# Pairing two chunks of the q·k products by accumulating DMA before the logit matmuls of a fused attention and gMLP kernel

## The chip, the cores and the metric

The kernel runs on one core of one Trainium2 chip. The metric is the device time of one execution in microseconds (us); lower is better. A run is quoted as the median of its executions. All comparisons use runs of the fast state; where a kernel also had executions in the slow state (e6_plain and e9_plainload), only the fast ones are quoted.

## The reference, cut to what matters

The input x (2048 tokens, 512 features, bf16) is normalised and then goes two ways at once, and both results are added to x:

```python
# A: attention with 32 heads of 16 features; each token sees 8 tokens, 2 apart
idx = pos[:, None] - arange(8) * 2
logits = einsum('bhsd,bhswd->bhsw', q, kg) * scale      # dot products over 16 features
attn = softmax(where(mask, logits, -1e9))
o = einsum('bhsw,bhswd->bhsd', attn, vg) @ wo
# B: gMLP
z = gelu(xn @ w_in); z1 = z[..., :688]; z2 = layernorm(z[..., 688:])
g = einsum('ts,bsf->btf', w_sp, z2) + b_sp              # w_sp is 2048 x 2048
out = x + o + (z1 * g) @ w_out
```

The change concerns only the logits. The large matmul with w_sp, called `pg` in the kernel, comes after them on the same engine.

## The kernel before

q and k come out of TensorE with the features on the 128 partitions, in four chunks of 128 features (8 heads each). VectorE multiplies q by shifted k. TensorE then sums the 16 features of each head: it multiplies the products by a 0/1 matrix `rsel`, and each chunk has its own matrix, which puts its 8 heads into its own 8 of 32 output rows. The four chunks add up in PSUM. The work is split into eight groups (four token blocks, two halves of the window), `prods(g)` and `logits(g)`.

```python
def qk_part(pq, j, c, b0, b1):                # chunk c of q (s=0) and k (s=1)
    for s in range(2):
        for kc in range(C):
            PE.matmul(pq[:, s, b0 * P:b1 * P], wqk[:, kc, s * D + c * P:s * D + (c + 1) * P],
                      xv[:, kc, b0:b1, j, :], start=(kc == 0), stop=(kc == C - 1))

def prod_w(g, ww):                            # one of four window positions, all four chunks
    V.tensor_tensor(pr[g % 2][:, :, ww], q4, k4, ALU.mult)

def logits(g):
    for c in range(C):                        # C = 4
        for tb in range(TB):                  # TB = 4
            PE.matmul(pl[32 * tb:32 * tb + 32, :, :], rsel[:, c, :], pr[g % 2][:, c, :, tb, :],
                      start=(c == 0), stop=(c == C - 1), tile_position=(0, 32 * tb))
    A.activation(lg[...], pl[:], ACT.Copy, scale=float(DH) ** -0.5)

# ... (the order of issue, cut)
SP.dma_start_transpose(b16[:], B_b_sp...)     # the bias column, late in the SyncE queue
G.tensor_copy(b_col[:], b16[:])               # GpSimd: waits for it
for c in range(C):
    prod_c(0, c)                              # groups 0 and 1, chunk by chunk
    prod_c(1, c)
# ...
logits(7)
add_mask()
sm_max(1)
z2s(3, 1)
z2s(3, 2)
for n in range(NWSP):
    load_wsp(n)                               # six DMA transposes of w_sp, from SyncE
# ...
```

`r_qk` holds q and k, and the w_sp tiles are written over it later: so the first six transposes wait until VectorE has made the last products.

## Time and profile before

The median is 210.8 us (210.47 to 211.88) before the prediction.

| read from | number |
|---|---|
| page, busy time | PE 202.7 of 209.3 us, 97% |
| page, chain | PE 93% of the span |
| groups | logit matmuls `pl`, 128 of them, 8.2 us |
| chain | `pg` starts at 83.5 us; PE is busy without gaps from there |
| timelines | GpSimd casts the bias at 35.9 us; w_sp transposes go out from 69.5 us |

From the page of the kernel before. First the span and the busy time by engine; then the span in 40 slices of 5.2 us, each digit the busy share in tenths (`PEclk`: the granted TensorE clock); then the chain of work that ended last, by engine; then two groups (line, engine, operation, out<-in, count, busy us, mean ns, and idle time before them with its releaser):

```profile
span 209.3 us, 4186 instructions
...
PE 202.7 (97%) x1727; PEld 121.3 (58%) x1731; DVE 176.9 (85%) x267; ACT 92.9 (44%) x148; POOL 5.7 (3%) x21
...
PE   7799999999999999999999999999999999999993
...
PEclk9999999999999999999999999999999999999999
DMA  4984556000000499799999776994833234424153
...
PE 93%; DMA 3%; SPq 2%; issue 1%; DVE 0%; DVEq 0%
...
L297 DVE TENSOR_TENSOR r_pr<-r_qk 128x2048 bf16<-128x2048 bf16 x24 | 27.5, 1218 | 2.8 <-ACT r_qk L269 2.8
L264 PEld LDWEIGHTS <-r_w 128*128 128x128 bf16 x176 | 16.8, 98 | 11.5 <-issue 1.8
```

TensorE is the limit, at full clock. The DMA row is empty between about 37 and 68 us: that is the room in which the change wants to work. VectorE, which makes the products, is the next engine (85%).

From the groups of the same trace, the logit matmuls, in the same columns:

```profile
L304 PE MATMUL pl<-r_pr,rsel 128*32 128x512 bf16 x128 | 8.2, 381 | 0.0
```

Nothing waits here, so 8.2 us is all that logit matmuls can give back, and half of it is what the change is after.

From the chain in order of time (start us, us, what), the stretch up to `pg`:

```profile
69.43 2.44 PE pz L207 x16
72.85 3.61 PE pz L207 x24
76.45 7.07 PE pv L342 x128
83.52 18.77 PE pg L377 x128
```

From the timelines of GpSimd and of SyncE (start us, us, engine, line, operation, count, idle time before and releaser):

```profile
35.92 1.05 POOL L540 CAST b_col<-b 128x16 f32<-128x16 bf16 x1 [30.43 <-DMA b<-in_B_b_sp_dram]
...
69.51 16.15 SPq L369 DMA_TRANSPOSE r_qk<-in_B_w_sp_dram  x6
```

The cast waits 30 us for its DMA and delays nobody. The six transposes go out the moment the last products are read.

### The profile page before, as it was taken

Reading aid. Unit: us, or ns where it says so; the run is one execution under the profiler, and the core shown is the slowest. Engines: PE = TensorE matmul, PEld = TensorE weight load, DVE = VectorE, ACT = ScalarE, POOL = GpSimd, SP = SyncE. Lnnn points to the kernel's source line nnn. Section 1 sums busy time; section 2 is a strip of 40 time slices with the busy share of each in tenths; the row PEclk is TensorE's granted clock in tenths of the full one; section 3 lists DMA queues with packets and bytes.
Section 4 is the critical chain, followed back from the end, with each engine's and each line's share of the span. In section 5 each row is a group of like instructions: output and inputs, shape, how many; then the busy total and the mean of one; then the engine's idle time right before and its main releaser. Section 6 shows DMA issues by size and latency. Waiting matters only on the chain.

```text
span 209.3 us, 4186 instructions
## 1 busy us (share of the span) xinstructions
PE 202.7 (97%) x1727; PEld 121.3 (58%) x1731; DVE 176.9 (85%) x267; ACT 92.9 (44%) x148; POOL 5.7 (3%) x21
## 2 busy tenths in 40 slices
PE   7799999999999999999999999999999999999993
PEld 2578644545566566666666666456666446664441
DVE  3888997969999987999999999859999979991404
ACT  3475797788997897941431223102123102231000
POOL 7000001100000000000000000000000000000000
PEclk9999999999999999999999999999999999999999
DMA  4984556000000499799999776994833234424153
GB/s 132 326 281 66 101 94 232 0 0 3 0 3 0 103 179 210 146 280 216 177 191 218 129 161 145 147 194 150 126 76 89 47 94 150 47 45 89 51 152 100
DMA packets 66914, 25.91 MB, mean 124 GB/s; under 512 B 56080, under 2 KB 66768, under 8 KB 66768
## 3 DMA queue, kind: packets, MB, share of 16 engines
q1 hardware_dynamic: 66304, 25.20, 56.1%
q10 hardware_dynamic: 592, 0.46, 0.7%
q8 instruction: 13, 0.21, 0.4%
q14 instruction: 5, 0.04, 0.1%
HBM read 10.13 MB, written 2.10 MB: 58 GB/s over the span
## 4 chain that ended last, share of the span: by engine, by line
PE 93%; DMA 3%; SPq 2%; issue 1%; DVE 0%; DVEq 0%
PE pg L377 36%; PE pz L207 18%; PE pq L264 12%; PE po L430 7%; PE po L411 7%; PE pv L342 7%; PE pl L304 4%; DMA r_w<-in_A_wqkv_dram 3%; PE pa L430 1%; PE po L417 1%; SPq L138 1%; SPq L131 1%; SPq L147 0%; PE pt L193 0%; DVE r_qk L422 0%
## 5 line engine op out<-in xcount | busy, mean ns | idle before, releaser
L377 PE MATMUL pg<-z,r_qk 128*128 128x344 bf16 x512 | 76.8, 309 | 0.0
L377 PEld LDWEIGHTS <-r_qk 128*128 128x128 bf16 x512 | 50.0, 98 | 24.9 <-issue 0.4
L207 PE MATMUL pz<-w_z,xnT 128*128 128x344 bf16 x256 | 40.9, 309 | 0.0
L380 ACT ACTIVATE gs<-pg,b_col 128x688 bf16<-128x688 f32 x16 | 13.3, 832 | 57.0 <-PE pg L377 50.1
L353 DVE TENSOR_TENSOR r_pr<-r_x,r_w 128x2048 bf16<-128x2048 bf16 x32 | 38.1, 1221 | 0.3
L357 DVE TENSOR_TENSOR r_pr<-r_pr 128x2048 bf16<-128x2048 bf16 x28 | 33.8, 1219 | 0.1
L207 PEld LDWEIGHTS <-xnT 128*128 128x128 bf16 x256 | 24.6, 98 | 14.7 <-issue 2.0
L264 PE MATMUL pq<-xnT,r_w 128*128 128x256 bf16 (+1 forms) x176 | 29.4, 321 | 0.8 <-ACT xnT L197 0.7
L297 DVE TENSOR_TENSOR r_pr<-r_qk 128x2048 bf16<-128x2048 bf16 x24 | 27.5, 1218 | 2.8 <-ACT r_qk L269 2.8
L264 PEld LDWEIGHTS <-r_w 128*128 128x128 bf16 x176 | 16.8, 98 | 11.5 <-issue 1.8
L422 DVE TENSOR_TENSOR r_qk<-po,r_qk 128x512 bf16<-128x512 f32 x14 | 9.0, 686 | 15.6 <-PE po L430 15.6
L256 ACT ACTIVATE z1u<-pz 128x688 bf16<-128x688 f32 x16 | 11.9, 742 | 20.8 <-PE pz L207 20.7
L269 ACT CAST r_qk<-pq 128x1024 bf16<-128x1024 f32 x16 | 15.8, 1012 | 5.8 <-PE pq L264 4.3
L430 PE MATMUL po<-r_w,uT 128*128 128x512 bf16 x66 | 14.9, 379 | 0.6 <-issue 0.6
L342 PE MATMUL pv<-xnT,r_w 128*32 128x512 bf16 x256 | 14.7, 380 | 0.0
L411 PE MATMUL po<-r_lg,r_pr 32*128 32x512 bf16 x224 | 14.5, 375 | 0.0
L430 PEld LDWEIGHTS <-uT 128*128 128x128 bf16 x80 | 7.5, 98 | 10.2 <-issue 1.7
L175 DVE BATCH_NORM_STATS2 stats<-r_x 128x6 f32<-128x512 bf16 x16 | 10.8, 672 | 2.3 <-DMA r_x<-in_A_x_dram 2.1
L219 ACT ACTIVATE junk<-z 128x688 bf16<-128x688 bf16 x16 | 12.4, 778 | 0.5
L213 ACT ACTIVATE z<-pz 128x688 bf16<-128x688 f32 x16 | 11.8, 736 | 1.9 <-PE pz L207 1.9
L342 PEld LDWEIGHTS <-r_w 128*32 128x32 bf16 x256 | 9.5, 139 | 4.5 <-issue 0.3
L411 PEld LDWEIGHTS <-r_pr 32*128 32x128 bf16 x256 | 6.2, 93 | 7.7 <-issue 1.3
(67 smaller groups left out, 136.3 us busy)
## 6 DMA issues: line engine op xcount, KB each, us to landing
r_lg<-in_A_wo_dram SPq DMA_DIRECT2D x4, 512.0 KB, 9.0
r_qk<-in_A_x_dram SPq DMA_DIRECT2D x16, 128.0 KB, 2.2
out_dram<-r_qk SPq DMA_DIRECT2D x15, 128.0 KB, 1.7
r_x<-in_A_x_dram SPq DMA_DIRECT2D x3, 512.0 KB, 6.0
w_z<-in_B_w_in_dram SPq DMA_DIRECT2D x2, 688.0 KB, 5.3
r_w<-in_A_wqkv_dram SPq DMA_DIRECT2D x4, 256.0 KB, 6.4
r_w<-in_B_w_out_dram SPq DMA_DIRECT2D x1, 640.0 KB, 5.6
r_w<-in_A_wqkv_dram SPq DMA_DIRECT2D x1, 512.0 KB, 4.0
```

Of the source, the lines that this page charges most:

```text
L207: PE.matmul(pz[:, hh, 0:FHALF], xnT[:, kc, i * P:(i + 1) * P], wz[:, kc, hh * FHALF:(hh + 1) * FHALF], start=(kc == 0), stop=(kc == C - 1))
L219: A.activation(junk[:], z2[:, i, :], ACT.Square, accum_out=zsq[:, q:q + 1])
L264: PE.matmul(pq[:, s, b0 * P:b1 * P], wqk[:, kc, s * D + c * P:s * D + (c + 1) * P], xv[:, kc, b0:b1, j, :], start=(kc == 0), stop=(kc == C ...
L269: A.copy(dst[:, :, :, j, :], pq[:].rearrange("p s (b t) -> p s b t", b=TB))
L297: V.tensor_tensor(pr[g % 2][:, :, ww], q4, k4, ALU.mult)
L342: PE.matmul(pv[32 * tb:32 * tb + 32, dd, :], wv[:, kc, 2 * d2 + dd, :], xnT[:, kc, tb * TBS:(tb + 1) * TBS], start=(kc == 0), stop=(kc == ...
L353: V.tensor_tensor(pw_t[n], vp[:, :, off:off + P], a_sb[:, slot_w(w), ts].unsqueeze(1).broadcast_to([P, DH, P]), ALU.mult)
L357: V.tensor_tensor(pw_t[n] if dst is None else dst, pw_t[n], pw_t[m], ALU.add)
L377: PE.matmul(pg[:, hh, 0:FHALF], wsp[n % NWSP][:, k, :], z2[:, k, hh * FHALF:(hh + 1) * FHALF], start=(q == 0), stop=(q == NT - 1))
L380: A.activation(gs[:], pg[:, :, 0:FHALF], ACT.Identity, bias=b_col[:, i:i + 1])
L411: PE.matmul(pos[tb], op[32 * tb:32 * tb + 32, d, o * P:(o + 1) * P], wo_r[32 * tb:32 * tb + 32, d, :], start=(d == 0), stop=False, tile_po ...
L430: PE.matmul(pos[tb], uT[:, o % 2, m, tb * P:(tb + 1) * P], wout[:, m, :], start=False, stop=(m == MCH - 3))
```

## The change: its intent and its diff

If the features are dealt to chunks by stride 4 (chunk c takes features c, c+4, c+8, ...), then every chunk holds four features of every head, all four chunks need the same 0/1 matrix, and chunks may be added before it. An accumulating DMA, issued by GpSimd, adds chunks 2 and 3 to chunks 0 and 1 inside SBUF. The logits then need 8 matmuls a group, not 16. To give the DMAs time, a third product buffer is made and the logits are moved later in TensorE's order. Core of the diff:

```diff
-    pr = [r_pr[:, n * 8192:(n + 1) * 8192]... for n in range(2)]
+    pr_home = [r_pr[:, 0:8192], r_pr[:, 8192:16384], r_uz[:, (NZ1 + 8) * FPAD - 8192:]]   # three buffers
+    pr = [h.rearrange("p (w c b t) -> p w c b t", w=4, c=C, b=TB) for h in pr_home]
 # load order: all of q, then all of k, then x block 1 (before: half of q and k, x block 1, the other half)
     load_wqk(SP, 0)
+    load_wqk(SP, 1)
     SP.dma_start(xall[:, 1], xblk[1])
-    load_wqk(SP, 1)
 # qk_part
-                PE.matmul(..., wqk[:, kc, s * D + c * P:s * D + (c + 1) * P],
+                PE.matmul(..., wqk[:, kc, s * D + c:(s + 1) * D:C],
+    def pair_c(g, c):
+        p = pr[g % 3]
+        G.dma_start(p[:, :, c].rearrange("p w b t -> p w (b t)"),
+                    p[:, :, c + 2].rearrange("p w b t -> p w (b t)"), accum_op=ALU.add)
+    def pair_w(g, w0):
+        p = pr[g % 3][:, w0:w0 + 2].rearrange("p w c b t -> p w (c b t)")
+        G.dma_start(p[:, :, 0:1024], p[:, :, 1024:2048], accum_op=ALU.add)
 # logits
-        for c in range(C):
+        for c in range(2):
-                PE.matmul(..., rsel[:, c, :], pr[g % 2][:, c, :, tb, :], start=(c == 0), stop=(c == C - 1), ...)
+                PE.matmul(..., rsel[:], pr[g % 3][:, :, c, tb, :], start=(c == 0), stop=(c == 1), ...)
 # prods: after every second window position
+            if ww % 2:
+                pair_w(g, ww - 1)
 # order of issue (start)
     for c in range(C): qk_mm(2, c)
-    logits(0)
-    logits(1)
     prods(2)
-    prods(3)
     qk_mm(3, 0) ... qk_mm(3, 2)
+    logits(0)
+    logits(1)
+    prods(3)
 # ... the later logits move back in the same way; v_mm and z1_mm pieces are moved ahead of them (cut)
```

More of the change, by code (lines that the diff above doesn't have):

```diff
@@ L99 @@
     r_pr = sb.tile([P, 2 * 4 * C * TB * P], BF16, name="r_pr")
-    pr = [r_pr[:, n * 8192:(n + 1) * 8192].rearrange("p (c w b t) -> p c w b t", w=4, c=C, b=TB) for n in range(2)]
+    r_uz = sb.tile([P, (NZ1 + 8) * FPAD], BF16, name="r_uz")
+    z1u = r_uz[:, 0:NZ1 * FPAD].rearrange("p (n f) -> p n f", n=NZ1)
+    uT = r_uz[:, NZ1 * FPAD:(NZ1 + 8) * FPAD].rearrange("p (s m t) -> p s m t", s=2, m=MCH)
+    pr_home = [r_pr[:, 0:8192], r_pr[:, 8192:16384], r_uz[:, (NZ1 + 8) * FPAD - 8192:]]
+    pr = [h.rearrange("p (w c b t) -> p w c b t", w=4, c=C, b=TB) for h in pr_home]
     pw_t = [r_pr[:, n * 2048:(n + 1) * 2048].rearrange("p (d t) -> p d t", d=DH) for n in range(4)]
@@ L107 @@
     z2 = sb.tile([P, NT, FH], BF16, name="z2")
-    z1u = sb.tile([P, NZ1, FPAD], BF16, name="z1u")
     smt = sb.tile([P, 4, 256], F32, name="smt")
-    uT = sb.tile([P, 2, MCH, TBS], BF16, name="uT")
     ident = sb.tile([P, P], BF16, name="ident")
-    rsel = sb.tile([P, C, 32], BF16, name="rsel")
+    rsel = sb.tile([P, 32], BF16, name="rsel")
     mask = sb.tile([32, W, HALO], F32, name="mask")
@@ L133, in load_wqk @@
     def load_wqk(E, h):
-        w = wqk.rearrange("p k (s c f) -> p k s c f", s=2, c=C)
-        src = A_wqkv[:, 0:2 * D].rearrange("(k p) (s c f) -> p k s c f", p=P, s=2, c=C)
-        for s in range(2):
-            E.dma_start(w[:, :, s, 2 * h:2 * h + 2, :], src[:, :, s, 2 * h:2 * h + 2, :])
+        src = A_wqkv[:, 0:2 * D].rearrange("(k p) f -> p k f", p=P)
+        E.dma_start(wqk[:, :, h * D:(h + 1) * D], src[:, :, h * D:(h + 1) * D])
     load_x0(SP, 0, 0, 64)
@@ L160 @@
     G.memset(rsel[:], 1.0)
-    for c in range(C):
-        G.affine_select(out=rsel[:, c, :], in_=rsel[:, c, :], compare_op=ALU.is_ge, fill=0.0,
-                        base=128 * c, pattern=[[-16, 32]], channel_multiplier=1)
-        G.affine_select(out=rsel[:, c, :], in_=rsel[:, c, :], compare_op=ALU.is_ge, fill=0.0,
-                        base=15 - 128 * c, pattern=[[16, 32]], channel_multiplier=-1)
+    G.affine_select(out=rsel[:], in_=rsel[:], compare_op=ALU.is_ge, fill=0.0,
+                    base=0, pattern=[[-4, 32]], channel_multiplier=1)
+    G.affine_select(out=rsel[:], in_=rsel[:], compare_op=ALU.is_ge, fill=0.0,
+                    base=3, pattern=[[4, 32]], channel_multiplier=-1)
     G.memset(mask[:], 0.0)
@@ L169 @@
                         fill=NEG, base=-DIL * slot_w(4 * h), pattern=[[DIL, 4], [1, HALO]], channel_multiplier=0)
-    G.memset(z1u[:, :, FH:FPAD], 0.0)
+    G.memset(z1u[:, 0:7, FH:FPAD], 0.0)
     def ln_stats(i):
@@ L263, in qk_part @@
             for kc in range(C):
-                PE.matmul(pq[:, s, b0 * P:b1 * P], wqk[:, kc, s * D + c * P:s * D + (c + 1) * P],
+                PE.matmul(pq[:, s, b0 * P:b1 * P], wqk[:, kc, s * D + c:(s + 1) * D:C],
                           xv[:, kc, b0:b1, j, :], start=(kc == 0), stop=(kc == C - 1))
@@ L286, in prod_c @@
         k4 = bass.AP(k3.tensor, k3.offset, [list(x) for x in k3.ap[0:2]] + [[DIL, 4], list(k3.ap[2])])
-        V.tensor_tensor(pr[g % 2][:, c].rearrange("p w b t -> p b w t"),
+        V.tensor_tensor(pr[g % 3][:, :, c].rearrange("p w b t -> p b w t"),
                         q3.unsqueeze(2).broadcast_to([P, TB, 4, P]), k4, ALU.mult)
@@ L296, in prod_w @@
         k4 = qk[:, :, 1, off:off + S].rearrange("p c (b j t) -> p c b j t", b=TB, j=4)[:, :, :, j, :]
-        V.tensor_tensor(pr[g % 2][:, :, ww], q4, k4, ALU.mult)
+        V.tensor_tensor(pr[g % 3][:, ww], q4, k4, ALU.mult)
+    def pair_c(g, c):
[5 more added lines that the diff above has]
+        G.dma_start(p[:, :, 0:1024], p[:, :, 1024:2048], accum_op=ALU.add)
     def logits(g):
@@ L301, in logits @@
         pl = ps_aux.tile([P, 4, P], F32, name="pl", tag="aux")
-        for c in range(C):
+        for c in range(2):
             for tb in range(TB):
-                PE.matmul(pl[32 * tb:32 * tb + 32, :, :], rsel[:, c, :], pr[g % 2][:, c, :, tb, :],
-                          start=(c == 0), stop=(c == C - 1), tile_position=(0, 32 * tb))
+                PE.matmul(pl[32 * tb:32 * tb + 32, :, :], rsel[:], pr[g % 3][:, :, c, tb, :],
+                          start=(c == 0), stop=(c == 1), tile_position=(0, 32 * tb))
         A.activation(lg[:, 4 * h:4 * h + 4, o, :], pl[:], ACT.Copy, scale=float(DH) ** -0.5)
@@ L543 @@
         prod_c(1, c)
+        if c >= 2:
+            pair_c(0, c - 2)
+            pair_c(1, c - 2)
     z2s(0, 0)
@@ L555 @@
     qk_mm(3, 2)
+    logits(0)
+    logits(1)
+    prods(3)
     z2s(0, 3)
-    logits(2)
     qk_mm(3, 3)
@@ L560 @@
     prods(4)
+    logits(2)
+    v_mm(0)
+    z2s(1, 1)
+    z2s(1, 2)
     logits(3)
@@ L564 @@
     sm_sub(0)
-    v_mm(0)
-    z2s(1, 1)
-    z2s(1, 2)
+    v_mm(1)
+    z2s(1, 3)
+    z2s(2, 0)
     logits(4)
@@ L570 @@
     G.memset(vp[0:32, :, 0:HALO], 0.0)
-    v_mm(1)
-    z2s(1, 3)
-    z2s(2, 0)
+    v_mm(2)
+    z2s(2, 1)
+    z2s(2, 2)
     logits(5)
     prods(7)
-    v_mm(2)
-    z2s(2, 1)
-    for n in range(4):
-        z1_mm(n)
-    z2s(2, 2)
+    v_mm(3)
+    z1_mm(0)
+    z1_mm(1)
+    z2s(2, 3)
+    z1_mm(2)
+    z2s(3, 0)
+    z2_stat_dve(0, 1)
     logits(6)
-    z2_stat_dve(0, 1)
-    v_mm(3)
-    z2s(2, 3)
-    z2s(3, 0)
+    v_mm(4)
+    z2s(3, 1)
+    z2s(3, 2)
     logits(7)
@@ L588 @@
     sm_max(1)
-    z2s(3, 1)
-    z2s(3, 2)
+    v_mm(5)
+    z2s(3, 3)
     for n in range(NWSP):
         load_wsp(n)
-    z2s(3, 3)
-    v_mm(4)
+    z1_mm(3)
+    v_mm(6)
     z2_stat_dve(2, 3)
     sm_sub(1)
-    for d2 in range(5, 8):
-        v_mm(d2)
+    v_mm(7)
     SP.dma_start(vp[32:P, :, 0:HALO], vp[0:P - 32, :, TBS:TBS + HALO])
```

## The prediction

> **What bounds it now.** TensorE. The profile page gives PE 202.7 of 209.3 us busy (97%); the table by windows shows it busy 10.00 of every 10 us from 30 to 130 us at full granted clock; the chain of waits is 93% PE. VectorE is close behind: 28.15 of 30 us busy between 40 and 70 us.
>
> **What the change removes.** Logit matmuls (pl). In the chain each group of 16 takes 0.98 us; eight groups are 3.7% of the span, 7.8 us. Eight matmuls per group save 0.49 us a group, 3.9 us in all. If nothing else moved: 206.9 us.
>
> **What it adds.** Sixteen GpSimd-issued accumulating DMAs of 512 KB source each. None is in this trace, so I estimate. An add reads both operands (the Trainium skill, "Collectives: The Full Stack", Part 3: two reads, one write), so 1.05 MB is read per DMA: 3.2 us at the best rate of the DMA row of this trace, 326 GB/s; 2.4 us at 435 GB/s, the fabric ceiling of "DMA: Bandwidth & Descriptors", Specifications. That page's "Anatomy of one DMA" adds about 2 us fixed. VectorE makes one half group in 2.44 us (two products of 1.22 us), so the DMAs are no faster than their producer.
>
> **What it moves.**
> 1. GpSimd runs in order. Its b_col cast stands ahead of the first accumulating DMA; now it waits 30.4 us for the b DMA, until about 35.9 us, then takes 1.05 us. So the four DMAs of groups 0 and 1 leave at about 37 us, although their products are ready at 31 to 34.6 us.
> 2. TensorE reaches the first logits at about 39.6 us (summing chain pieces in the new order). Group 0 needs the third DMA: 37+2+3x2.4 to 3.2, 46 to 48.5 us. Group 1: 48.5 to 52 us. TensorE idles about 9 us there.
> 3. Products of group 3 need the buffer of group 0, and the last q/k block's last copy stands behind these logits on TensorE, so VectorE slips too: the last products end about 75 to 80 us, against 69.4 now.
> 4. The last logits wait for the last DMA (which meets the w_sp transposes started by the same products); 7.5 us of TensorE work follow before the pg matmuls: these start at 88 to 98 us, against 83.5. From there TensorE is busy without gaps, so the delay stays.
>
> Side terms: all of wqk must land before the first k half (about 0.4 us lost, but the wait at 11.3 us goes); x block 1 lands about 1 us later. Stride-4 weight loads: this trace has 32-column loads at 32-byte stride at 139 ns against 96 ns contiguous; at 8 bytes I expect about 98 ns, hidden.
>
> **Prediction.** 219 us, 80% range 210.5 to 232. Faster by over 2%: 0.04; within 2%: 0.21; slower by over 2%: 0.75.
>
> **What would show each step.** Groups: pl x64, about 3.9 us. GpSimd timeline: cast at about 36 us, accumulating DMAs after it. TensorE timeline: gaps of several us before the first two pl groups, released by DMA, smaller ones later. Chain: DMA r_pr several per cent. DMA row filled from 37 to 85 us. pg starting near 90 us. pq LDWEIGHTS about 98 ns; pg, pz, pv, po durations unchanged.
>
> **What would make it wrong.** An accumulating DMA that costs like a plain copy (1.2 us each at the ceiling): then about 210 us. Slower generation or adding (4 us or more each): over 230. A TensorE clock that falls after idling adds a few us. Weight loads over 107 ns would show on the 96 256-column pq matmuls.

## The result, and the profile after

The changed kernel took 240.83 us (median of four, 240.42 to 243.62) against 210.93 us for the kernel before on the same chip. Kernels are compared only within the same rounds. The ratio of the fast runs is 1.144, with a 95% interval of 1.138 to 1.151. Here and below a ratio is the mean time of one kernel's fast runs over that of the other's in the same rounds, so it is not quite the ratio of the medians. The change costs 14%: the direction was predicted, but the time lies outside the stated range (210.5 to 232).

From the page of the changed kernel, the same parts, and two more: the DMA queue that GpSimd fills (packets, MB, share of the 16 engines) and the issue of the adds (count, KB each, median us from issue to landing):

```profile
span 238.0 us, 4100 instructions
...
PE 204.3 (86%) x1667; PEld 123.2 (52%) x1667; DVE 177.5 (75%) x267; ACT 93.5 (39%) x148; POOL 23.8 (10%) x31
...
PE   7799997129968982089999999999999999999994
...
PEclk9999999656999999569999999999999999999999
DMA  5953574999897999999898799767844614433243
...
q0 software_dynamic: 5376, 8.39, 23.0%
...
PE 58%; DMA 19%; DVE 15%; issue 3%; SPq 2%; POOL 2%; ACT 1%; DVEq 0%; POOLq 0%
...
L296 DVE TENSOR_TENSOR r_pr<-r_qk 128x2048 bf16<-128x2048 bf16 x16 | 18.4, 1221 | 14.2 <-PE pl L312 10.3
L312 PE MATMUL pl<-r_pr,rsel 128*32 128x512 bf16 x48 | 5.2, 498 | 26.5 <-DMA r_pr<-r_pr 25.9
L263 PEld LDWEIGHTS <-r_w 128*128 128x128 bf16 x176 | 19.5, 114 | 10.2 <-DMA r_w<-in_A_wqkv_dram 1.5
...
r_pr<-r_pr POOLq DMA_DIRECT2D x12, 512.0 KB, 8.0
```

The PE row now has two holes, around 45 us and around 96 us. The clock row falls in the same places: TensorE also comes back slower. The DMA row is nearly full from about 40 to 110 us. TensorE waited 25.9 us for the adds, and its busy time rose by 1.6 us although 64 matmuls are gone. The first of these waits also holds up VectorE: it sat 10.3 us, in one piece, until a logit matmul released its product buffer.

From TensorE's timeline of the changed kernel (idle time before a piece and its releaser in brackets):

```profile
43.64 0.62 PE L312 MATMUL pl<-r_pr,rsel 128*32 128x512 bf16 x4 [3.67 <-DMA r_pr<-r_pr]
50.46 1.04 PE L312 MATMUL pl<-r_pr,rsel 128*32 128x512 bf16 x8 [6.21 <-DMA r_pr<-r_pr]
53.27 0.62 PE L312 MATMUL pl<-r_pr,rsel 128*32 128x512 bf16 x4 [1.76 <-DMA r_pr<-r_pr]
...
71.79 0.61 PE L312 MATMUL pl<-r_pr,rsel 128*32 128x512 bf16 x8 [2.55 <-DMA r_pr<-r_pr]
...
102.29 1.04 PE L312 MATMUL pl<-r_pr,rsel 128*32 128x512 bf16 x8 [11.75 <-DMA r_pr<-r_pr]
...
111.97 1.19 PE L385 MATMUL pg<-z,r_qk 128*128 128x344 bf16 x7
```

Two stretches carry most of the loss: 11.6 us of waiting at the first two groups (3.67 + 6.21 + 1.76), and 11.75 us at the last one. `pg` starts at 111.97 us, not at 83.5. After that the kernels take the same time, 126.0 and 125.8 us, so the 28.5 us that are lost at `pg` are nearly the whole growth of the span (28.7 us).

From its timelines of GpSimd and of SyncE:

```profile
36.47 1.00 POOL L550 CAST b_col<-b 128x16 f32<-128x16 bf16 x1 [32.55 <-DMA b<-in_B_b_sp_dram]
37.41 5.31 POOL L300 DMA_DIRECT2D r_pr<-r_pr  x4
...
82.87 1.19 POOL L305 DMA_DIRECT2D r_pr<-r_pr  x1 [0.86 <-DVE zm L224]
...
82.64 29.72 SPq L377 DMA_TRANSPOSE r_qk<-in_B_w_sp_dram  x6
```

The cast stands ahead of the first adds, as predicted. The last add is issued 0.2 us after the first transpose: both wait for the same last product, which ends at 82.57 us (the profile names a small VectorE instruction on `zm` that runs just then; neither transfer uses it). Issuing the six transposes took 29.7 us, against 16.15 us before.

From its chain in order of time:

```profile
39.80 13.42 DMA r_pr<-r_pr
53.89 2.41 PE pz L206 x8
...
82.87 19.29 DMA r_pr<-r_pr
102.29 1.04 PE pl L312 x8
```

The last add took 19.3 us from issue to landing; the median of the twelve on that buffer is 8.0. The `pz` piece after the first hole took 2.41 us for the eight matmuls that take 1.17 us elsewhere. Here the Trainium skill helps to read the clock row: "TensorE: Matmul & The Clock Gate", Part 1, says that the idle default is a throttled clock at half rate, and that activity releases it. This trace agrees: the granted clock was 0.53 between 43 and 54 us, during and after the first waits, and 0.50 between 96 and 105 us, around the end of the last one.

### The profile page after: what moved, and what is told of

Its sections match the earlier page's. It is cut to its first block, busy times and chain, and to the rows that moved or that the text cites. A ratio compares the mean times of both kernels' runs of the same rounds, so it can differ in the third digit from the quotient of the medians.

```text
span 238.0 us, 4100 instructions
## 1 busy us (share of the span) xinstructions
PE 204.3 (86%) x1667; PEld 123.2 (52%) x1667; DVE 177.5 (75%) x267; ACT 93.5 (39%) x148; POOL 23.8 (10%) x31
## 4 chain that ended last, share of the span: by engine, by line
PE 58%; DMA 19%; DVE 15%; issue 3%; SPq 2%; POOL 2%; ACT 1%; DVEq 0%; POOLq 0%
PE pg L385 31%; DMA r_pr<-r_pr 14%; PE pz L206 8%; PE po L438 7%; PE po L419 6%; DVE r_pr L296 4%; DVE stats L174 3%; DMA r_x<-in_A_x_dram 3%; PE pv L350 3%; DMA b<-in_B_b_sp_dram 2%; DVE r_uz L296 2%; DVE r_x L185 2%; DVE r_pr L286 1%; PE pq L263 1%; DVE mv L175 1%
## 5 line engine op out<-in xcount | busy, mean ns | idle before, releaser
L206 PE MATMUL pz<-w_z,xnT 128*128 128x344 bf16 x256 | 42.3, 315 | 0.3 <-ACT r_qk L268 0.3
L296 DVE TENSOR_TENSOR r_pr<-r_qk 128x2048 bf16<-128x2048 bf16 x16 | 18.4, 1221 | 14.2 <-PE pl L312 10.3
L312 PE MATMUL pl<-r_pr,rsel 128*32 128x512 bf16 x48 | 5.2, 498 | 26.5 <-DMA r_pr<-r_pr 25.9
L263 PEld LDWEIGHTS <-r_w 128*128 128x128 bf16 x176 | 19.5, 114 | 10.2 <-DMA r_w<-in_A_wqkv_dram 1.5
L255 ACT ACTIVATE r_uz<-pz 128x688 bf16<-128x688 f32 x16 | 11.9, 742 | 20.7 <-PE pz L206 20.7
L312 PEld LDWEIGHTS <-rsel 128*32 128x32 bf16 x64 | 1.3, 98 | 30.6 <-issue 20.9
L350 PE MATMUL pv<-xnT,r_w 128*32 128x512 bf16 x256 | 16.1, 398 | 0.0
L438 PE MATMUL po<-r_w,r_uz 128*128 128x512 bf16 x70 | 15.8, 380 | 0.0
L314 ACT ACTIVATE r_lg<-pl 128x512 f32<-128x512 f32 x8 | 4.7, 589 | 23.9 <-PE pl L312 23.9
L212 ACT ACTIVATE z<-pz 128x688 bf16<-128x688 f32 x16 | 11.8, 740 | 3.3 <-PE pz L206 3.3
L350 PEld LDWEIGHTS <-r_w 128*32 128x32 bf16 x256 | 10.2, 141 | 5.3 <-issue 1.9
```

The lines of the kernel that those rows point to most:

```text
L206: PE.matmul(pz[:, hh, 0:FHALF], xnT[:, kc, i * P:(i + 1) * P], wz[:, kc, hh * FHALF:(hh + 1) * FHALF], start=(kc == 0), stop=(kc == C - 1))
L263: PE.matmul(pq[:, s, b0 * P:b1 * P], wqk[:, kc, s * D + c:(s + 1) * D:C], xv[:, kc, b0:b1, j, :], start=(kc == 0), stop=(kc == C - 1))
L296: V.tensor_tensor(pr[g % 3][:, ww], q4, k4, ALU.mult)
L350: PE.matmul(pv[32 * tb:32 * tb + 32, dd, :], wv[:, kc, 2 * d2 + dd, :], xnT[:, kc, tb * TBS:(tb + 1) * TBS], start=(kc == 0), stop=(kc == ...
L438: PE.matmul(pos[tb], uT[:, o % 2, m, tb * P:(tb + 1) * P], wout[:, m, :], start=False, stop=(m == MCH - 3))
```

## The experiments

The theory after reading the traces had three parts. (a) At the tail, the last add meets the transposes and is slowed by them. (b) At the start, the bias cast delays the first adds. (c) The adds are slow enough by themselves to make TensorE wait. The rivals: the strided weight loads or the new order cost the time; the adds would be too slow with or without the transposes; any traffic, or the place in memory, would do the same.

Times are medians; every ratio is to the kernel before in the same rounds.

| run | time, us | ratio, 95% interval |
|---|---|---|
| changed kernel | 240.83 | 1.144 (1.138 to 1.151) |
| e1_hold: transposes wait for the last add | 228.21 | 1.083 (1.080 to 1.087) |
| e2_cast: cast after the adds | 233.7 | 1.110 (1.106 to 1.114) |
| e3_both | 223.43 | 1.061 (1.056 to 1.065) |
| e5_nodma: no adds (wrong result) | 209.4 | 0.993 (0.990 to 0.997) |
| e6_plain: copies in place of adds (wrong result) | 221.1 (two fast runs; two slow ones took 225) | 1.049 (1.045 to 1.053) |
| e9_plainload: plain loads beside the last adds | 233.89 (one fast run; the other, 237.8, was slow) | no ratio |
| e4_stride: before + stride and load order | 212.01 | 1.008 (1.005 to 1.012) |
| e8_order: before + load order | 211.85 | 1.005 (1.000 to 1.010) |
| e10_qfirst: e4 + q halves first | 212.68 | 1.008 (1.006 to 1.011) |
| e11_late / e12_early: before + two adds | 215.67 / 216.33 | 1.023 / 1.026 (see text) |
| e13_adds2 / e15_inplace: before + two adds | 210.69 / 210.87 | 0.998 / 1.000 |
| e14_adds4 / e16_behind: before + four adds | 213.91 / 213.28 | 1.013 / 1.012 |
| h1 / h2: only groups 2 to 5 paired | 213.5 / 211.55 | 1.014 / 1.004 |

### e1_hold: the transposes may not start before the last add has landed

```diff
+    hold = sb.tile([P, 2], BF16, name="hold")
 # before the first six load_wsp
+    SP.dma_start(hold[:], pr[7 % 3][:, 3, 0, 0, 0:2])     # 4 bytes a partition, out of the last add's result
```

> The changed kernel, with one small SP transfer that reads what the last accumulating DMA writes, so that the first six w_sp transposes are issued only after it has landed. Theory (transposes and accumulating DMAs starve each other): the last accumulating DMA lands 6 to 8 us after its issue instead of 19.3, the last logits start near 90 us instead of 102.3, pg near 99 us instead of 112, total 226 to 230 us. Rival (the last DMA was slow by itself[...]): it still takes 15 us or more and the total stays at 238 us or more.

It ran in 228.21 us: 12.6 us of the loss are gone. From its timelines of TensorE and SyncE:

```profile
91.57 0.62 PE L313 MATMUL pl<-r_pr,rsel 128*32 128x512 bf16 x8
...
99.90 13.30 PE L386 MATMUL pg<-z,r_qk 128*128 128x344 bf16 x90
...
91.39 0.53 SPq L609 DMA_DIRECT2D hold<-r_pr  x1
92.02 15.44 SPq L378 DMA_TRANSPOSE r_qk<-in_B_w_sp_dram  x6
```

The last add was issued at 83.60 us, about as before, and had landed by 91.4 us: under 8 us in place of 19.3. TensorE no longer waits at the last logits, and `pg` starts at 99.90 us although the transposes leave 9 us later than in the changed kernel. They are now issued in 15.4 us. So part (a) is shown: taking the transposes away from the last add takes the long landing away. A rival, that VectorE's work held the add up, fails on the trace: in the changed kernel VectorE had no instruction between 88.8 and 104.0 us, and the adds were slow all through 88 to 96 us.

### e2_cast and e3_both: the bias cast moves behind all the adds

```diff
-    G.tensor_copy(b_col[:], b16[:])      # ahead of the first products
 # before the first six load_wsp
+    G.tensor_copy(b_col[:], b16[:])
```

> The changed kernel with the b_col cast moved behind all accumulating DMAs in GpSimd's order. Theory (the cast held the first four DMAs back): the first one is issued at 31 to 32 us instead of 37.4, the first logits of group 0 no longer wait until 50.5 us but until about 45, products end 4 to 6 us earlier, total 234 to 237 us with the collision at the end still there. Rival (the DMAs' own throughput sets the pace from the start, so an earlier start is lost): total within 1 us of 240.8.

The first adds were issued at 32.43 us, not 37.41; group 0's logits came at 46.01 us (50.46) and group 1's at 48.62 us (53.27); the time fell by 7.1 us to 233.7 us. The last add was still in flight from 79.0 to 95.7 us, 16.7 us. That is just under the 234 to 237 us expected. Part (b) is shown.

e3_both holds the transposes and moves the cast.

> Both edits, the held transposes and the cast moved. Theory: the gains add, about 12 us and 5 us, total 221 to 225 us. That is still slower than the kernel before, since sixteen transfers at 2.8 to 3.3 us each follow the products. If the total is under 213 us, the DMAs' throughput is no limit of its own; if over 228, one of the two causes is not one.

It took 223.43 us, 4.8 us less than e1_hold. The two gains, 12.6 and 7.1 us alone, make 17.4 us together, so they add up for the most part, but not wholly. From its TensorE timeline:

```profile
47.58 1.04 PE L313 MATMUL pl<-r_pr,rsel 128*32 128x512 bf16 x8 [5.38 <-DMA r_pr<-r_pr]
50.10 0.62 PE L313 MATMUL pl<-r_pr,rsel 128*32 128x512 bf16 x4 [1.48 <-DMA r_pr<-r_pr]
...
68.68 0.61 PE L313 MATMUL pl<-r_pr,rsel 128*32 128x512 bf16 x8 [2.60 <-DMA r_pr<-r_pr]
...
87.19 0.61 PE L313 MATMUL pl<-r_pr,rsel 128*32 128x512 bf16 x8 [0.45 <-DMA r_pr<-r_pr]
...
95.51 17.67 PE L386 MATMUL pg<-z,r_qk 128*128 128x344 bf16 x120
```

With both causes gone there are still 10.2 us of waits for adds (these four and one of 0.28 us). That is part (c).

### e5_nodma: the same program without the adds

```diff
     def pair_c(g, c):
-        G.dma_start(..., accum_op=ALU.add)
+        return
     def pair_w(g, w0):
-        G.dma_start(..., accum_op=ALU.add)
+        return
```

> The changed kernel without the sixteen accumulating DMAs; half of the products is lost, so the result is wrong on purpose. It shows what two chunks instead of four in the logits are worth when the additions are free. Theory (TensorE-bound, VectorE close behind): pg starts 2 to 4 us before the 83.5 us of the kernel before; with the later start that the stride-4 kernel showed, 207 to 210 us. Rival (VectorE's products bind, so fewer matmuls give nothing): 211 us or more.

The logits then lack half of their terms: the result is wrong. The time was 209.4 us, 0.7% under the kernel before. From its groups:

```profile
L263 PE MATMUL pq<-xnT,r_w 128*128 128x256 bf16 (+1 forms) x176 | 30.6, 331 | 1.5 <-DMA r_w<-in_A_wqkv_dram 0.9 <-ACT xnT L196 0.7
...
L311 PE MATMUL pl<-r_pr,rsel 128*32 128x512 bf16 x48 | 3.5, 383 | 0.0
...
L311 PE MATMUL pl<-r_uz,rsel 128*32 128x512 bf16 x16 | 1.2, 384 | 0.0
```

This bounds the idea. Even additions that cost nothing are worth 1.3 us. The logit matmuls fell from 8.2 to 4.7 us, but the q/k matmuls `pq` rose from 29.4 to 30.6 us and TensorE waited 0.9 us for wqk, so 3.5 - 1.2 - 0.9 = 1.4 us are left. Everything between 209.4 and 223.4 us (e3_both), 14.0 us, is the adds themselves: 10.2 us of waits, TensorE working 3.7 us longer (204.2 us busy against 200.5) for the same matmuls, as the granted clock in its page falls after the waits.

### e6_plain: GpSimd-issued copies of the same bytes in place of the adds

```diff
-        G.dma_start(..., accum_op=ALU.add)
+        G.dma_start(...)                      # overwrites: wrong result on purpose
```

> The changed kernel with plain copies in place of the accumulating DMAs, same shapes, issued from GpSimd too; wrong result on purpose. Theory (an addition reads two operands, so it takes about twice as long as a copy): 2 KB packets near 90 to 100 ns instead of 188, 512 KB in about 1.5 us, the first logits wait 3 to 6 us less, total 222 to 232 us. Does the end collide as well? If the starvation by the transposes belongs to accumulation, the last copy lands within 6 us; if to any GpSimd-issued transfer beside transposes, it takes over 10 us. Rival (fixed cost of GpSimd-issued transfers, not the reading of two operands, sets the time): total within 3 us of 240.8.

Its fast runs took 221.1 us, just under the expected range. A copy's 4096-byte packet took 172 ns; an add's packet of 2048 bytes took 188 ns and one of 1024 bytes 114 ns. In bytes of the source, copies ran at up to 380 GB/s, adds with 2 KB rows at about 185 and with 1 KB rows at about 165 GB/s (182 in e3_both), so in the changed kernel a 512 KB add occupies the engines for 2.8 or 3.2 us. The Trainium skill, "Collectives: The Full Stack", Part 3, says of the adding step of a collective that it reads two sources for one write and so reaches half the rate of the copying step; that it holds for adds inside SBUF too is what these rates show, 185 against 380. GpSimd also needed 1.2 us to issue an add and 0.7 us to issue a copy. Copies at half the price save 19.7 us of the changed kernel's time, and still lose 5% against the kernel before: the late cast, the fixed time of each DMA and the meeting with the transposes stay. The last copy, issued at 78.27 us, landed 7.9 us later, where each of the three copies before it took 3.1 us, and TensorE waited 4.09 us for it. That is neither the 6 us nor the 10 us of the expectation: the transposes slow copies as well, but less than adds. The profiled execution of this run counts as slow, while two of its timed runs are fast; only durations are taken from that profile.

### e9_plainload: is it any traffic, or the transposes?

```diff
 # the transposes held as in e1_hold; in their old place, plain loads of the same 512 KB tiles
+    for n in range(NWSP):
+        SP.dma_start(r_qk[:, n * 2048:(n + 1) * 2048], B_w_sp[tile_of(n) * P:(tile_of(n) + 1) * P, :])
+    SP.dma_start(hold[:], pr[7 % 3][:, 3, 0, 0, 0:2])
```

> The kernel with held transposes (228.2 us), but in the place where the transposes used to start there are six ordinary 512 KB loads of the same rows from HBM, which the held transposes overwrite later. Theory (it is the transposes that starve and are starved): with ordinary loads beside them the last accumulating DMA lands within 8 to 13 us of its issue, as two queues that share the engines fairly. Rival (any heavy traffic on SyncE's queue does it): 16 us or more.

The last add was issued at 83.07 us and had landed by 95.7 us: 12.6 us, against 7.7 us alone (e1_hold) and 19.3 us beside the transposes. So about 5 of the 11.6 us come with plain traffic as well; the rest is the transposes' own. The loads slow the add in a different way, too. The packet records of this and four other cases, in stretches in which the queues named had work:

```
what runs together              stretch, us   add packets (2 KB)   other packets        adds, other, GB/s
e9_plainload: adds + loads      84 to 95      517                  503 of 4096 B        96, 187
changed kernel: adds + transp.  88 to 96      46                   1142 of 256 B        12, 37
e2_cast: adds + transposes      88 to 95      222                  685 of 256 B         65, 25
e1_hold: adds alone             82 to 90      724                  none                 185, 0
before: transposes alone        72 to 84      none                 9170 of 256 B        0, 196
```

(The 4-byte packets, 16 for each add, and a few of 16 KB on another queue are left out.) Plain loads and adds go through in almost equal numbers of packets, 503 to 517, which fits what the Trainium skill says in "DMA: Bandwidth & Descriptors", section on queues, rings and completion order, under arbitration: each engine goes round robin between its queues at packet granularity. The counts of adds and transposes do not look like this: 46 to 1142 and 222 to 685. (A record of the trace need not be a packet in the page's sense.) In the changed kernel both together moved 49 GB/s where either alone moves 185 or 196, and transpose packets took a median of 99 ns against 18 ns alone. The same state shows in e2_cast between 86 and 90 us: adds at 13 and transposes at 27 GB/s.

### e11_late and e12_early: two adds in the kernel before, beside the transposes or without them

```diff
 # the kernel before
+    G.memset(uf[:, 0:4096], 0.0)                # uf: uT, flat
+    def two_adds():
+        for n in range(2):
+            G.dma_start(uf[:, n * 2048:(n + 1) * 2048]..., r_pr[:, 8192 + n * 2048:...]..., accum_op=ALU.add)
+    two_adds()      # e11_late: with the transposes; e12_early: at 62 us, where the DMA engines are idle
```

> The kernel before with just two 512 KB accumulating DMAs added, into memory that nothing reads before it is overwritten, issued when the last products are ready, which is also when the six w_sp transposes start. Theory (the two kinds starve each other, whoever uses the result): the second one lands 12 us or more after its issue, moving under 50 GB/s for most of that, and the transposes slow down too. Rival (the late landing in the changed kernel came from its own backlog or from work that waits for it): it lands within 9 us of its issue.

> The same two accumulating DMAs, issued in the kernel before after the products of group 5, when no other DMA runs. Both theories: the first lands 6 us and the second 8 to 9 us after the first one's issue, at about 185 GB/s; total at most 1 us longer than the kernel before. It is the control of the late pair.

The landings say something: beside the transposes the two adds landed 8.2 and 10.5 us after issue, alone 5.3 and 8.1 us, and the transposes' issue took 21.5 us in place of 16.15. The totals say nothing about the adds, because both kernels had lost time long before them: in e12_early the first `pz` matmul started at 29.13 us, not at 23.54. From the timelines of e12_early:

```profile
5.08 4.00 DVE L188 TENSOR_SCALAR r_x<-r_x,mv,rstd 128x512 bf16<-128x512 bf16 x1
...
5.43 3.50 POOL L172 MEMSET uT<- 128x4096 bf16 x1
```

One VectorE instruction took 4.00 us here that otherwise takes 0.41 us: it began during the GpSimd memset that stands before the added one, and ended 0.15 us after the added one did. The Trainium skill, "SBUF — State Buffer", section "Who interferes with whom", describes this: VectorE and GpSimd share a pair of ports, which one of them holds exclusively while its instruction runs (for VectorE only in some instructions, `tensor_scalar` among them); the two lines agree. So the expected small cost of e12_early failed for a cause that the experiment brought in itself: without the memset two adds cost nothing (e13_adds2, below).

### e13_adds2, e14_adds4, e15_inplace, e16_behind: without the memset, more adds, another place, another order

```diff
 # the kernel before, ahead of the six load_wsp (e16_behind: after them)
+    def adds(k):                                # d, f: the two product buffers
+        for n in range(k):
+            G.dma_start(d[:, w0:w0 + 2, x0:x0 + 1024], f[:, w0:w0 + 2, x0:x0 + 1024], accum_op=ALU.add)
+    adds(2)    # e13_adds2; adds(4) in e14_adds4 and, into f, in e16_behind
 # e15_inplace: source in the same buffer, 2 KB further on, as in the changed kernel
```

> The isolated collision again, without the long GpSimd memset that spoiled the start of the first pair: in the kernel before, two 512 KB accumulating DMAs in rows of 2 KB (the changed kernel's shape, not merged to 4 KB) start with the w_sp transposes; they add into a buffer that is dead by then. Theory (the 2 KB shape is what falls into the slow state): the second lands 14 us or more after issue. Rival (two transfers are too few, a backlog of four is needed): about 10 us, as with the 4 KB rows (10.5).

> The same with four of them, about the backlog that the changed kernel has when its transposes start. Alone they would take 2.9 + 4 x 2.8, about 14 us to the last landing. Theory (transposes and queued adds slow each other in total): the last lands 19 us or more after its issue, and the stretch in which both are in flight moves under 100 GB/s together. Rival (they only take turns): 14 to 17 us, with the transposes pushed back by as much as the adds take.

> The isolated pair of 2 KB rows again (second landing 10.9 us after issue), but source and destination 2 KB apart in one buffer, as in the changed kernel, instead of 16 KB apart. Theory (the addresses bring the slow state): 14 us or more. Rival (they don't matter): 10 to 12 us.

> The isolated four adds again (last landing 14.7 us after its issue, begun 2 us ahead of the transposes), but issued only after the last logits, at about 73 us, when the transposes have been in flight for some 3 us, as the last add of the changed kernel came in after its transposes had been issued. Theory (what comes second behind a stream of transposes gets a small share): last landing 19 us or more after its issue, with a stretch of several us in which both move under 100 GB/s together. Rival (order does not matter, they take turns): 13 to 17 us.

Two adds cost the program nothing (210.69 us; in place 210.87 us). Four cost 1.3 and 1.2%. From the SyncE timeline of e14_adds4, and then of e16_behind:

```profile
69.13 25.90 SPq L369 DMA_TRANSPOSE r_qk<-in_B_w_sp_dram  x6
```

```profile
69.52 26.35 SPq L369 DMA_TRANSPOSE r_qk<-in_B_w_sp_dram  x6
```

The transposes are delayed by about 10 us by four adds, whether these are issued ahead of them or 3.2 us after them. Here the two kinds take turns: between 76 and 82 us of e14_adds4 the adds ran at 193 GB/s, their full rate, and the transposes at 9 GB/s; in e16_behind, between 78 and 88 us, 180 and 11 GB/s. The last of four adds landed 14.7 and 14.4 us after issue. Adding in place instead of between buffers made no difference (5.5 and 9.5 us against 6.4 and 10.9 us). How long would these adds take alone? An estimate of 2.9 us fixed and 2.83 us for each add puts the last landing 8.6 us (two adds) or 14.2 us (four) after the first issue. Measured were 11.8 and 10.3 us for two (e13_adds2, e15_inplace), and 17.4 and 16.7 us for four (e14_adds4, e16_behind). So the transposes lengthen the landing in every arrangement tried, but by 2 to 3 us, and not by the 11.7 us of the changed kernel. The forecasts of 14 us and 19 us for the slow state failed. The stretch of the changed kernel in which both were slow together appeared in none of these four; what brings that state about stays open.

### e4_stride, e8_order, e10_qfirst: the weights dealt by stride, and the load order

```diff
 # e4_stride: the kernel before, still with four chunks and no adds, plus
+        E.dma_start(wqk[:, :, h * D:(h + 1) * D], src[...])       # all of q, then all of k, then x block 1
+                PE.matmul(..., wqk[:, kc, s * D + c:(s + 1) * D:C], ...)
 # e8_order: only the load order.  e10_qfirst: e4_stride, first three q halves ahead of the k halves
```

> The kernel before with only the dealing by stride 4: strided weight loads, one 0/1 matrix for all chunks, and the new order of the first loads; four chunks in the logits, no accumulating DMA. Theory (harmless): 210.3 to 211.8 us, pq weight loads at most 115 ns, no gap on TensorE by them. Rival (strided loads cost time where 256-column matmuls leave none to hide them, or x block 1 comes later and stays late): over 212 us.

> The kernel before with only the new order of the first loads (all q columns of wqk, all k columns, then x block 1), contiguous chunks and unstrided weight loads. Theory (the loss of 0.8% of the stride-4 kernel is that of the loads): 211.7 to 212.7 us. Rival (it is the strided weight loads): 210.3 to 211.1 us.

> The stride-4 kernel without accumulating DMAs (212.0 us) with another order of its first matmuls: the q halves of three chunks first, then their k halves, so that TensorE has work until the second half of wqk has landed. Theory (the loss of 1.2 us came from the wait for that half and the lower granted clock after it): 210.3 to 211.2 us, no wait for wqk. Rival (it came from the strided weight loads, 116 against 98 ns): it stays at 211.7 us or more.

e4_stride was 0.8% slower. In its profile TensorE waited 0.7 us for wqk, and its first matmuls then ran at a lower clock (0.57 between 8 and 12 us). A strided weight load took 116 ns in the mean, a contiguous one 98 ns. Did that cost time? From the TensorE timelines of the kernel before and of e4_stride, the same 72 matmuls with their weight loads:

```profile
13.98 9.73 PE L264 MATMUL pq<-xnT,r_w 128*128 128x256 bf16 x72
15.48 9.73 PE L262 MATMUL pq<-xnT,r_w 128*128 128x256 bf16 x72
```

At full clock the slower loads cost nothing; the 1.5 us were lost before, in the start. The Trainium skill, "TensorE: Matmul & The Clock Gate", section on weight-path perf modes, gives the read pattern of the fast weight load as packed or strided, without a difference; here there is one of 18%, though no trace shows whether these loads are of that kind. The load order alone (e8_order) cost 0.5%, with an interval of 0.0 to 1.0, so most of the loss may lie there; the intervals overlap, and the shares stay open. e10_qfirst should have bridged the wait for wqk with the q halves, and gave nothing (1.008). But in its profile TensorE waited 2.4 us for wqk, more than before: the idea was not carried out by this edit, and the run doesn't decide between its two theories.

### h1 and h2: pair only where there is time

h1 pairs only groups 2 to 5, which are neither behind the cast nor ahead of the transposes; the other four groups keep 16 matmuls. h2 also issues q halves first and moves the logits of groups 3 and 4 later.

```diff
+PAIRED = (2, 3, 4, 5)
 # logits
+        n = 2 if g in PAIRED else C
+        for c in range(n):
 # prods
+            if ww % 2 and g in PAIRED:
+                pair_w(g, ww - 1)
```

> A hybrid: chunks dealt by stride 4, but only groups 2 to 5 are added by DMA, where neither the first wait nor the transposes meet them; their logits are moved about 5 us later on TensorE, the other four groups keep four chunks. Theory (with the DMAs hidden, only the 4 x 0.49 us of matmuls and the 1.2 us of the stride-4 start remain): pg starts 0.5 to 1 us before the kernel before, 209 to 210.7 us. Rival (the DMAs' throughput or an overlooked wait still binds): over 212 us.

> The hybrid with that order of the first matmuls, and with the logits of groups 3 and 4 moved 1 to 2 us further back, where the first hybrid waited 0.84 and 1.11 us for landings. Theory (these waits and the start made it slower than the kernel before): no waits for DMA at the logits, 209 to 210.5 us, a little faster than the kernel before. Rival (VectorE's chain to the normalised z2 sets the end of this stage): 211 us or more with no wait at the logits.

Both expectations were missed: 213.5 and 211.55 us, ratios 1.014 and 1.004. In h1's profile the start is late again (the first `pz` at 26.82 us, 23.54 in the kernel before), and two waits for adds cost 1.9 us. In h2 almost nothing waits for an add (one wait of 0.68 us), and `pg` starts at 83.74 us. So the long waits can be avoided, but then the saving is only 32 matmuls, about 2 us, and `pg` still starts 0.2 us later than before. Of what eats the saving, 0.6 us are seen at the start (the first logits at 33.76 us, 33.12 before) and 0.7 us at the wait; the rest is not assigned. VectorE, the rival of the expectation, is not it: no wait of TensorE for VectorE stands between the first logits and `pg`. From the groups of h2, each shape apart:

```profile
L266 PE MATMUL pq<-xnT,r_w 128*128 128x256 bf16 x96 | 11.6, 273 | 1.3 <-ACT xnT L199 0.7 <-DMA r_w<-in_A_wqkv_dram 0.7
```

273 ns is also the mean of these matmuls in the kernel before: here too the slower weight loads stay hidden. No version that was run beats the kernel before with a right result.

## Why the prediction was right or wrong, point by point

| step, as the prediction put it | predicted | measured |
|---|---|---|
| first four adds leave after the cast | about 37 us | 37.41 us |
| one 512 KB add occupies the engines | 2.4 to 3.2 us | 2.8 us (2 KB rows), 3.2 us (1 KB rows) |
| its fixed time | about 2 us | about 2.9 us |
| TensorE reaches the first logits | 39.6 us | 40.0 us (43.64 less the wait of 3.67) |
| group 0, group 1 logits | 46 to 48.5, 48.5 to 52 us | 50.46, 53.27 us |
| last products end | 75 to 80 us | 82.6 us |
| last products to last logits | 5.5 to 10.5 us (88 - 7.5 - 75 to 98 - 7.5 - 80) | 19.7 us |
| TensorE from last logits to `pg` | 7.5 us | 9.7 us |
| `pg` starts | 88 to 98, near 90 us | 111.97 us |
| from there to the end | unchanged | unchanged |
| stride-4 weight load | about 98 ns, hidden | 114 ns, hidden at full clock |

**What was right.** The direction, the place behind the cast, the price of one add, the chain of delays (logits late, buffer late, products late, `pg` late), and that a delay at `pg` is carried to the end. The estimate from two reads for one write held. e2_cast and e3_both show the start as it was argued.

**The step that failed is number 4**, "The last logits wait for the last DMA (which meets the w_sp transposes started by the same products)". It saw the meeting, but gave it no time of its own. An estimate shows how much: the last four adds of the changed kernel were issued from 76.30 us, so with 2.9 us fixed and 4 x 2.83 us they would land at 90.5 us; they landed at 102.2 us. The same sum for e1_hold, from 77.03 us, gives 91.3 us, and 91.4 was measured. So the adds by themselves need 8 us after the last products, inside the predicted span, and the meeting adds 11.7 us. e1_hold measures 12.6 us of time for it, more than half of the 22 us by which the prediction missed. That the transposes are the cause is shown by e1_hold; why they slow an add so much just here is not.

**The rest is terms that were too small**, all in the same direction. The fixed time was taken from the Trainium skill, "DMA: Bandwidth & Descriptors", "Anatomy of one DMA", at about 2 us; this trace has about 2.9 us (the first add was issued at 37.41 us and the matmul that waited for it started at 43.64 us; less 3.2 us of transfer and 0.1 us for the release, 2.9 us remain; GpSimd's 1.2 us of issuing are in it). It is paid before the first logits. With the 1 KB rows of the first four adds it made those logits 1 to 2 us later than the late end of the range; the products ended 2.6 us after theirs. TensorE's work between the last logits and `pg` was 2.2 us longer than the 7.5 us of the prediction. In e1_hold, where nothing waits there and the granted clock is 1.00, it took 8.3 us: so 1.4 us of the 2.2 are the lower clock after idling (named as a risk, but given no time in the sum), and 0.8 us an estimate that was too short. Measured against the late end of the predicted `pg` (98 us), 2.6 us come from the products, 9.2 us from the last DMA and 2.2 us from the work after it: 14.0 us, the distance to 111.97.

**Right in kind, too large in size:** the saving. "If nothing else moved: 206.9 us" is 3.9 us less than 210.8. e5_nodma measures 1.3 us, because 64 matmuls were 3.5 us and the start gives 2.1 us back (the `pq` matmuls and the wait for wqk). Also, a DMA as cheap as a plain copy was expected to give about 210 us; e6_plain took 221 us, since cheaper bytes leave the cast, the fixed time and the transposes where they are.

**What stays open:** why adds and transposes fell to 49 GB/s together in the changed kernel (and to 40 in e2_cast), and only took turns when the same adds were put into the kernel before; and how the 0.8% of e4_stride divides between load order and the rest of the start.

## What to carry to other kernels

Before giving work to an asynchronous helper, ask what stands ahead of it in its issuing engine's order, how long its last result takes from issue to landing, and what else the same event sets free on the DMA engines; price the meeting, not only the transfer. Bound the gain first with a run in which the helper is free: here it was 1.3 us, less than the 2.9 us of fixed time of a single add, so that one add left uncovered would be enough to lose it. When TensorE is made to wait, add the slower clock of the work after the wait (here 1.4 us at the last logits).

## What the Trainium skill lacked or had wrong

- Accumulating DMAs against DMA transposes ("DMA: Bandwidth & Descriptors", arbitration): adds and plain loads go through in equal numbers of packets (517 to 503), as the page lets one expect; the records of adds and transposes do not (46 to 1142). Four adds ran at 180 to 193 GB/s and left transposes 9 to 11 GB/s; in the changed kernel both fell to 12 and 37 GB/s, and one 512 KB add took 19.3 us to land.
- The rate of an add inside SBUF by row size, which I found on no page: about 185 GB/s of source bytes with 2 KB rows, 165 to 182 GB/s with 1 KB rows, against up to 380 GB/s for a copy, whose packets are of 4 KB; GpSimd's time to issue one is 1.2 us against 0.7 us for a copy.
- The fixed time of a GpSimd-issued DMA ("DMA: Bandwidth & Descriptors", "Anatomy of one DMA"): about 2 us there, about 2.9 us here for an add. For a plain copy it was about 1.7 us (3.1 us from issue to landing, less 1.4 us at 380 GB/s), so one figure does not fit both.
- Weight loads by stride ("TensorE: Matmul & The Clock Gate", weight-path perf modes): packed and strided are named together, with no time for either; here a load of 128 columns 8 bytes apart took 113 to 116 ns against 98 ns contiguous. It stayed hidden behind the matmuls (72 of them took 9.73 us both ways).
